# Block 1 of a retention kernel computed as one chunk of 128 tokens, with the order of all steps written anew

## The chip, the cores and the metric

The kernel runs on one core of a Trainium2 chip. The metric is the device time of one execution in microseconds; lower is better. Three runs of the kernel before gave 430.15, 433.15 and 433.55 us, median 433.15. The profile is of one further execution, which took 432.04 us, with a span of 430.3 us from the program's first instruction to its last.

## The reference

Two stages follow each other. The first is a decayed linear attention (retention) over 4 batches, 8 heads, 768 tokens and 64 channels per head, written in the reference with blocks of 64 tokens:

```python
for b in range(nb):                          # nb = 12 blocks of 64
    intra = einsum('bhic,bhjc->bhij', qb, kb) * Dmask        # lam^(i-j) for i >= j
    intra = einsum('bhij,bhjd->bhid', intra, vb)
    inter = einsum('bhid,bhde->bhie', qb * lam_pow, kv_state)  # lam^(i+1)
    out[:, :, sl] = intra + inter
    kb_dec = kb * lam ** (block - 1 - pos)
    kv_state = lam ** block * kv_state + einsum('bhsd,bhse->bhde', kb_dec, vb)
```

The second mixes each token with the one before it (`xk = mu_k * x + (1 - mu_k) * x_prev`, the same for `xr`), and computes `sigmoid(xr @ w_r) * (relu(xk @ w_k)^2 @ w_v)` with a model width of 512 and a hidden width of 1024. The weights come in 64-bit floats, and all results are in 32-bit floats. The block length of the first stage is free: any chunk length gives the same values if the decay tables fit it.

## The kernel before

The 768 tokens go through in NT = 6 blocks of 128, the 8 heads in HP = 4 head pairs. One letter stands for each kind of step, then the block and the head pair or column group; a long string, `ORDER` (lines 483 to 508), lists all steps, and line 459 runs them in this order. Every engine keeps its own instructions in the order in which they are issued (`InOrder`, line 22), so the string sets the order on all five engines and on the load queue, which SyncE (SP) issues. Each engine works in order; a step waits for the data and the buffers that it needs.

Steps of the first stage, per block n and head pair hp:

- `L` (`load_hp`, line 93) and `N` (`load_qv`, line 100) load into one of two input tiles, `IN[hp % 2]`, which head pairs 0 and 2, and 1 and 3, share in turn. Columns 0 to 3 of a tile hold queries, values, keys by column and keys by row. In block 0 one transfer of 1 MB brings all four. In later blocks one of 512 KB brings the keys (`kk`) and two of 256 KB bring queries and values (`qv`); `M` (`clear`, line 108) sets to zero the halves of the tile that must be empty.
- `A` (`scores`, line 249): products of keys and queries into the `sc` tiles in PSUM. `a` (`decay`): VectorE multiplies them by the decay table `Dt` into the tile `mv`.
- `q` (`decay_queries`, line 288): VectorE scales the queries by the table `LP` into other rows of `mv`, in four instructions of 64x256. `k` (`decay_keys`): ScalarE scales the keys in place.
- `U` (`sums`): products of keys and values into `u`. `u` (`even_state`) and `w` (`odd_state`): the state `ST[hp]` is multiplied by a power of the decay and `u` is added; before each, ScalarE copies the state into the empty half of the value columns (`to_values`, line 319; four copies of 64x256 per pair and block).
- `B` (`values`, line 339): values times `mv` into `xp`, from which ScalarE and VectorE make the mixed inputs (`E`, `e`, `F`, `f`).

Block 0 treats its 128 tokens as one chunk: `scores` makes 8 products of 64 rows and 128 columns, `values` 8 products with a stationary tile of 128 rows by 64 columns and 128 moving columns; there is no state yet. Blocks 1 to 5 work in two halves of 64 tokens. The trick there is that the state is laid next to the values of the half, and the scaled queries next to the scores, so that one product of 128 rows gives intra and inter together: 8 products for `scores`, 16 of 64 moving columns for `values`, 8 for `sums`.

Steps of the second stage: `R` and `Q` (the sigmoid branch, two batches each), `s` (sigmoid), `K` (hidden products for one of 8 column groups), `h` and `p` (square and split), `V` (output products, two halves for each batch), `o` (output). Weights are loaded (`S`) as 64-bit numbers and turned to 32 bits on ScalarE, GpSimd and VectorE (`c`, `C`); for blocks 1 to 5 they are split in a high and a low part (`D`, and `x`, `y` for inputs), and each product is made of three quick passes. In block 0 the `R`, `Q` and `K` steps use one slow 32-bit product. `T0`, `T1` and `T2` (`powers`, line 155) make the tables `Dt` and `LP` by products, and `Z` steps (`keep_busy`, line 175) are filler products on zeros.

On TensorE a profile row counts two records for one 32-bit product.

Of the kernel before, what the change touches and what calls it, by code (L numbers as in the profile page):

```python
# [7 lines left out]
F32 = mybir.dt.float32  # L8
# [7 lines left out]
HP = H // 2  # L16
# [17 lines left out]
def tile_retention_moe(  # L34
    ctx: ExitStack,
    tc: tile.TileContext,
    qvk0: bass.AP,
# [50 lines left out]
    LP = const.tile([128, H, 64], F32, name="LP")  # L88
    LC = tiny.tile([128, HP], F32, name="LC")
# [3 lines left out]
    def load_hp(n, hp):  # L93
        t = IN[hp % 2]
        if n == 0:
            sync.dma_start(t[:, 0:4].rearrange("p c o -> p (c o)"), qvk0[hp])
            return
        sync.dma_start(t[:, 2:4].rearrange("p c o -> p (c o)"), kk[n - 1, hp])

    def load_qv(n, hp):  # L100
        t = IN[hp % 2]
        for i in range(2):
            rows, cols = slice(i * 64, i * 64 + 64), slice(i * 4, i * 4 + 2)
            sync.dma_start(t[rows, cols].rearrange("p c o -> p (c o)"), qv[n - 1, hp, rows])
# [3 lines left out]
    def clear(n, hp):  # L108
        t = IN[hp % 2]
        gpsimd.memset(t[64:128, 0 if n == 1 and hp < 2 else 1:2], 0.0)  # L110
        gpsimd.memset(t[0:64, 4 if n == 1 and hp < 2 else 5:6], 0.0)
# [6 lines left out]
    smalls = tiny.tile([128, 7 + H + 2 * HP], F32, name="smalls")  # L118
    sync.dma_start(smalls, small)
    rows = [work.tile([128, w], F32, tag="rt", name="rows", bufs=4) for w in (328, 200)]  # L120
    eye = rows[0][:, 200:328]
    sync.dma_start(rows[0], hot)
    lcol, ecol, lrow, erow, prow = (smalls[:, a:b] for a, b in ((0, 1), (1, 5), (5, 13), (13, 14), (14, 15)))
    mus = smalls[:, 7 + H:].rearrange("p (w c) -> p w c", w=2)
# [7 lines left out]
    lone = work.tile([128, 640], F32, tag="kf", name="lone")  # L132
    gpsimd.memset(lone[:, 512:640], 1.0)
# [13 lines left out]
    rows = rows[1]  # L147
    vector.tensor_scalar(omu, mus, -1.0, 1.0, op0=ALU.mult, op1=ALU.add)
# [6 lines left out]
    def powers(step):  # L155
        i = int(step[1])
        if i == 2:
            by_head = lone[:, 0:512].rearrange("p (h i) -> p h i", h=H)
            vector.tensor_tensor(by_head, rows[:, 72:136].rearrange("p (o i) -> p o i", o=1).broadcast_to([128, H, 64]),
                                 eye[:, 15::16].rearrange("p (h o) -> p h o", o=1).broadcast_to([128, H, 64]), op=ALU.mult)  # L160
            tensor.matmul(tables[2], lone[:, 512:640], lone[:, 0:512], start=True, stop=True)
            scalar.copy(LP.rearrange("p h i -> p (h i)"), tables[2])
            for ab in range(2):
                half = slice(ab * 64, ab * 64 + 64)
                gpsimd.tensor_copy(LC[half], LP[half, :, 63].rearrange("p (h a) -> p a h", a=2)[:, ab])
            return
# [82 lines left out]
    def scores(n, hp):  # L249
        q = Q[hp % 2]  # L250
        if n == 0:
# [19 lines left out]
    def decay(n, hp):  # L271
        sc, mv = scs.pop((n, hp)), mv_of(n, hp)
        if n == 0:
# [14 lines left out]
    def decay_queries(n, hp):  # L288
        q, mv = Q[hp % 2], mv_of(n, hp)
        for eo in range(2):  # L290
            dr = slice(64, 128) if eo == 0 else slice(0, 64)
            for ab in range(2):
                rows = slice(ab * 64, ab * 64 + 64)
                lp = LP[rows, 2 * hp + ab:2 * hp + ab + 1, :].broadcast_to([64, B, 64])
                vector.tensor_tensor(mv[dr, eo, :, ab, :], q[rows, ab, :, eo, :], lp, op=ALU.mult)

    def decay_keys(n, hp):
        kn = KN[hp % 2]
        for ab in range(2):
            h = 2 * hp + ab  # L300
            scalar.activation(kn[:, :, ab, :], kn[:, :, ab, :], AF.Copy, scale=(PW if n == 0 else KD)[:, h:h + 1])

    def sums(n, hp):
        kn, vs = KN[hp % 2], VS[hp % 2]
        us[n, hp] = u = ps_1.tile([128, B, 2, 64], F32, tag="u", name="u")
        for b in range(B):
            for ab in range(2):
                if n == 0:
# [14 lines left out]

    def even_state(n, hp):
        u, state = us[n, hp][:, :, 0, :], ST[hp]
        if n == 0:
            scalar.copy(state, u)
            return
        to_values(n, hp, 0, state)
        vector.scalar_tensor_tensor(state, state, LC[:, hp:hp + 1], u, op0=ALU.mult, op1=ALU.add)  # L330
        to_values(n, hp, 1, state)

    def odd_state(n, hp):
        vector.scalar_tensor_tensor(ST[hp], ST[hp], LC[:, hp:hp + 1], us.pop((n, hp))[:, :, 1, :],
                                    op0=ALU.mult, op1=ALU.add)

    def values(n, hp):
# [4 lines left out]
        for eo in range(1 if n == 0 else 2):  # L342
            for b in range(B):
                for ab in range(2):
                    rows = slice(ab * 64, ab * 64 + 64)
                    if n == 0:
                        tensor.matmul(xp[rows, b].rearrange("p e i -> p (e i)"), vs[:, 0, b, ab, :], mv[:, ab, b, :], start=True, stop=True)
# [136 lines left out]
Sr0 cr0 Cr0 Z10 T0 L00 Sr1 Z1 A00 k00 U00 a00 Z2 B00 cr1 L01 u00 Cr1 Sr2 k01 A01 a01 E00 U01 cr2 L02 u01 e00 T1 B01  # L484
Sr3 E01 L03 T2 F00 k02 Cr2 A02 f00 R00 e01 cr3 a02 U02 B02 M10 k03 u02 F01 f01 A03 Cr3 U03 Sk0 e02 R01 E02 a03 ck0 N10
L10 L11 Q00 f02 F02 R02 u03 Sk1 k10 q10 B03 N11 M11 Ck0 U10 E03 A10 Sk2 F03 Q01 R03 Q02 L12 e03 f03 ck1 u10 a10 B10
Sk3 N12 w10 Sv0 Sv1 M12 k11 U11 A11 s00 Ck1 Q03 s01 q11 E10 e10 ck2 k12 f10 u11 s02 K00 h00 a11 F10 A12 B11 M13 w11
L13 E11 Ck2 e11 a12 ck3 U12 K01 u12 f11 N13 K02 k13 s03 F11 Ck3 K03 w12 x10 cv0 A13 q12 B12 h01 h02 p00 h03 E12 N20
Sv2 Cv0 cv1 a13 L20 Dv0 U13 K04 u13 K05 Cv1 q13 K06 h04 p01 Dv1 K07 Sv3 M20 cv2 w13 A20 k20 U20 V00 h05 y10 L21 Cv2
k21 F12 e12 f12 V02 B13 h06 cv3 Dv2 M21 u20 Cv3 p02 N21 w20 h07 Dv3 p03 y11 x11 Dr0 V04 V06 q20 Dr1 U21 A21 V01 E13  # L490
V03 e13 V05 V07 o00 o01 a20 F13 f13 Dk0 B20 o02 o03 L22 y13 x12 R10 Q10 R11 Q11 R12 Q12 N22 u21 a21 x13 y12 Dk1 R13
Q13 L23 s10 q22 K10 s11 M22 E20 q21 K11 e20 s12 s13 w21 f20 F20 k22 U22 h10 A22 x20 Dk2 B21 K12 M23 a22 Dk3 K13 K14
h11 e21 N23 E21 F21 K15 h12 K16 p10 f21 h13 k23 u22 w22 B22 h14 U23 x21 A23 K17 p11 h15 E22 F22 u23 w23 V10 h16 y20
# [68 lines left out]
```

## Time and profile before

| | |
|---|---|
| runs, median (lowest to highest) | 433.15 us (430.15 to 433.55) |
| profiled execution | 432.04 us, span 430.3 us |
| granted TensorE clock, mean | 1.0 of full speed |
| TensorE matmul busy (records) | 419.5 us, 98% of the span (2935) |
| VectorE | 264.0 us, 61% |
| ScalarE | 204.9 us, 48% |
| GpSimd | 71.0 us, 16% |
| read from memory, written | 35.83 MB, 6.29 MB |

A profile row of a timeline gives the start in us from the span's beginning, the length in us, the engine, the line (all rows say L30, a helper), the operation, the tile written and those read, then for products the stationary tile's rows*columns, the output's partitions x columns, the count of records, and in brackets the idle time before it with what ended it. PE is TensorE's matmul, DVE VectorE, ACT ScalarE, POOL GpSimd, SPq SyncE's load queue. A grouped row gives after the bar the busy us in all, the mean ns of one, and the engine's idle time before such rows. A row of a window gives the stretch, its length, and busy us with the number of instructions for TensorE matmul, its weight loads, VectorE, ScalarE and GpSimd, then clock, share and GB/s of the transfers. Of matmuls the end is modelled, so the distance from one group's start to the next group's start is what it cost.

### The profile page before, as it was taken

How to read it: one execution, taken by the hardware profiler on the slowest of the kernel's cores; microseconds unless marked ns; L12 is line 12 of the kernel's file. 1: busy time of each engine (PE TensorE's matmuls, PEld its weight loads, DVE VectorE, ACT ScalarE, POOL GpSimd, SP SyncE). 2: the span in 40 equal slices, each digit the busy share in tenths (PEclk: the TensorE clock that was granted, in tenths of full speed). 3: DMA queues.
4: the chain of work that ended last, by engine and by line, in shares of the span. 5: the costliest groups of instructions: out<-in, count | busy, mean ns of one | idle time of the engine just before them, and what ended most of it. 6: DMA issues, size and time to landing. Idle time of an engine off the chain costs nothing.

```text
span 430.3 us, 7314 instructions
## 1 busy us (share of the span) xinstructions
PE 419.5 (98%) x2935; PEld 328.9 (76%) x2935; DVE 264.0 (61%) x402; ACT 204.9 (48%) x357; POOL 71.0 (16%) x142
## 2 busy tenths in 40 slices
PE   7998899999999999999999999999999999999996
PEld 4665545668888888888888888888878888888885
DVE  5886999979867674746667646555437561414411
ACT  3645686586677643344644434454244460224300
POOL 4366554331102011110020200000000000000000
PEclk9999999999999999999999999999999999999999
DMA  7889918131403213515004523004520001100001
GB/s 295 304 308 330 300 48 277 66 97 50 146 3 99 87 46 107 153 58 140 0 2 131 187 78 99 0 0 123 161 62 0 2 1 50 50 2 0 0 30 69
DMA packets 12306, 42.60 MB, mean 99 GB/s; under 512 B 1776, under 2 KB 2160, under 8 KB 10736
## 3 DMA queue, kind: packets, MB, share of 16 engines
q1 hardware_dynamic: 8672, 35.84, 26.5%
q10 hardware_dynamic: 3600, 6.29, 4.0%
q8 instruction: 23, 0.38, 0.4%
q14 instruction: 11, 0.09, 0.1%
HBM read 35.83 MB, written 6.29 MB: 98 GB/s over the span
## 4 chain that ended last, share of the span: by engine, by line
PE 81%; DVE 7%; DMA 6%; ACT 2%; POOL 1%; issue 1%; SPq 0%; DVEq 0%; ACTq 0%
PE vp L30 29%; PE kp L30 26%; PE rp L30 13%; PE xp L30 5%; PE sc L30 4%; DMA wst<-w_k 4%; PE u L30 3%; DMA in<-qv 2%; DVE wst L30 2%; DVE mv L30 1%; DVE lov L30 1%; PE table L30 1%; ACT wu L30 1%; DVE wu L30 1%; POOL wu L30 1%
## 5 line engine op out<-in xcount | busy, mean ns | idle before, releaser
L30 PE MATMUL vp<-hiv,k 128*128 128x512 f32 (+1 forms) x400 | 122.8, 384 | 1.0 <-ACT kf L30 1.0
L30 PEld LDWEIGHTS vp<-hiv,k 128*128 128x128 f32 x400 | 74.1, 188 | 16.9 <-ACT kf L30 1.4
L30 PE MATMUL vp<-lov,k 128*128 128x512 f32 (+1 forms) x200 | 76.2, 381 | 0.0
L30 PE MATMUL kp<-xh,hik 128*128 128x512 f32 x160 | 62.9, 393 | 0.0
L30 PE MATMUL kp<-xl,hik 128*128 128x512 f32 x160 | 62.3, 389 | 0.0
L30 PE MATMUL kp<-xh,lok 128*128 128x512 f32 x160 | 62.3, 389 | 0.0
L30 ACT ACTIVATE ts<-xp,omu 128x512 f32<-128x512 f32 x48 | 31.8, 684 | 62.5 <-PE xp L30 44.2
L30 DVE TENSOR_TENSOR kf<-kp,kf 128x512 f32<-128x512 f32 x40 | 27.4, 688 | 37.2 <-ACT kf L30 37.1
L30 ACT ACTIVATE kf<-kp 128x512 f32<-128x512 f32 x48 | 28.4, 594 | 37.6 <-PE kp L30 37.2
L30 ACT COPY in<-st 64x256 f32<-64x256 f32 x80 | 32.3, 404 | 22.1 <-DVE st L30 17.8
L30 PEld LDWEIGHTS vp<-lov,k 128*128 128x128 f32 x200 | 37.6, 188 | 6.9
L30 DVE TENSOR_TENSOR mv<-sc,Dt 64x512 f32<-64x512 f32 (+1 forms) x48 | 32.6, 686 | 12.3 <-PE sc L30 11.9
L30 DVE TENSOR_TENSOR xl<-ts,xh 128x512 fp32r<-128x512 f32 x40 | 27.7, 703 | 19.3 <-ACT xh L30 19.2
L30 DVE SCALAR_TENSOR_TENSOR ts<-xp,smalls,ts 128x512 f32<-128x512 f32 x40 | 29.6, 747 | 15.8 <-ACT ts L30 15.6
L30 DVE TENSOR_TENSOR mv<-in,LP 64x256 f32<-64x256 f32 x80 | 34.5, 431 | 3.2 <-DMA in<-qv 1.6
L30 DVE TENSOR_TENSOR k<-kf,k 128x1024 fp32r<-128x1024 f32 x24 | 29.1, 1223 | 10.7 <-ACT k L30 10.7
L30 DVE TENSOR_TENSOR rt<-vp,rt 128x512 f32<-128x512 f32 (+1 forms) x25 | 16.4, 665 | 31.5 <-PE vp L30 31.2
L30 PEld LDWEIGHTS kp<-xh,hik 128*128 128x128 f32 x160 | 30.0, 188 | 7.0 <-issue 0.9
L30 PEld LDWEIGHTS kp<-xh,lok 128*128 128x128 f32 x160 | 30.0, 188 | 6.3
L30 PEld LDWEIGHTS kp<-xl,hik 128*128 128x128 f32 x160 | 30.0, 188 | 6.0
L30 ACT CAST xh<-ts 128x512 fp32r<-128x512 f32 x40 | 24.1, 616 | 21.7 <-DVE rt L30 18.2
L30 DVE SCALAR_TENSOR_TENSOR st<-st,LC,u 128x256 f32<-128x256 f32 x36 | 17.2, 478 | 24.8 <-ACT in L30 20.0
(70 smaller groups left out, 586.3 us busy)
## 6 DMA issues: line engine op xcount, KB each, us to landing
in<-qv SPq DMA_DIRECT2D x40, 256.0 KB, 4.5
in<-kk SPq DMA_DIRECT2D x20, 512.0 KB, 4.6
out<-rt ACTq DMA_DIRECT2D x23, 256.0 KB, 2.0
in<-qvk SPq DMA_DIRECT2D x4, 1024.0 KB, 6.3
wst<-w_k SPq DMA_DIRECT2D x4, 1024.0 KB, 9.2
wst<-w_v SPq DMA_DIRECT2D x4, 1024.0 KB, 9.7
wst<-w_r SPq DMA_DIRECT2D x4, 512.0 KB, 7.1
out<-rt ACTq DMA_DIRECT2D x2, 128.0 KB, 1.7
```

The source lines that it names most:

```text
L30: return lambda *args, **kw: self.tc.keep_in_program_order(op(*args, **kw))
```

## The change

Block 1 is computed as block 0 is, as one chunk of 128 tokens, and adds what comes from the state by products of its own.

- **Loads.** The array `qvk` holds blocks 0 and 1; `L1x` is one transfer of 1 MB per head pair, and `N1x`, `M1x` are gone. The first clearing of both halves moves to block 2.
- **Scores, sums, decay.** In the forms of block 0. `scores` of block 1 takes two `sc` tiles instead of one.
- **Queries.** One VectorE instruction of 128x512 scales the queries in place, by `LP`, which is now laid out by head pair with 128 powers; `T2` makes it with another stationary tile (`pair`), and one VectorE instruction of 128x1 puts in the last power. Two GpSimd copies that made `LC` are gone; the state update reads its power from `LP`.
- **Values.** For each batch and head: one product as in block 0, then one with the stationary state (64 rows by 64 columns) and the scaled queries, added in PSUM. That is 8 + 8 products of 128 columns per pair.
- **State.** One VectorE instruction in place of two, and the four copies of `to_values` are gone in block 1.
- **Order.** The whole string `ORDER` is another one; two fillers (`Z2`) are gone.

```diff
     def load_hp(n, hp):
         t = IN[hp % 2]
-        if n == 0:
-            sync.dma_start(t[:, 0:4].rearrange("p c o -> p (c o)"), qvk0[hp])
-            return
-        sync.dma_start(t[:, 2:4].rearrange("p c o -> p (c o)"), kk[n - 1, hp])
+        if n < 2:
+            sync.dma_start(t[:, 0:4].rearrange("p c o -> p (c o)"), qvk[n, hp])
+            return
+        sync.dma_start(t[:, 2:4].rearrange("p c o -> p (c o)"), kk[n - 2, hp])
...
-        gpsimd.memset(t[64:128, 0 if n == 1 and hp < 2 else 1:2], 0.0)
+        gpsimd.memset(t[64:128, 0 if n == 2 and hp < 2 else 1:2], 0.0)
...
-    rows = [work.tile([128, w], F32, tag="rt", name="rows", bufs=4) for w in (328, 200)]
+    rows = [work.tile([128, w], F32, tag="rt", name="rows", bufs=4) for w in (456, 200)]
...
     def decay_queries(n, hp):
-        q, mv = Q[hp % 2], mv_of(n, hp)
+        q = Q[hp % 2]
+        if n == 1:
+            q = q[:, 0].rearrange("p b e i -> p b (e i)")
+            vector.tensor_tensor(q, q, LP[:, hp:hp + 1].broadcast_to([128, B, 128]), op=ALU.mult)
+            return
+        mv = mv_of(n, hp)
...
     def even_state(n, hp):
...
+        if n == 1:
+            vector.scalar_tensor_tensor(state, state, LP[:, hp, 127:128], u, op0=ALU.mult, op1=ALU.add)
+            return
...
     def values(n, hp):
...
-                    if n == 0:
-                        tensor.matmul(xp[rows, b].rearrange("p e i -> p (e i)"), vs[:, 0, b, ab, :], mv[:, ab, b, :], start=True, stop=True)
+                    if n < 2:
+                        x = xp[rows, b].rearrange("p e i -> p (e i)")
+                        tensor.matmul(x, vs[:, 0, b, ab, :], mv[:, ab, b, :], start=True, stop=n == 0)
+                        if n == 1:
+                            tensor.matmul(x, ST[hp][rows, b], Q[hp % 2][rows, 0, b].rearrange("p e i -> p (e i)"), start=False, stop=True)
...
 ORDER = """
-Sr0 cr0 Cr0 Z10 T0 L00 Sr1 Z1 A00 k00 U00 a00 Z2 B00 cr1 L01 u00 Cr1 Sr2 k01 A01 a01 E00 U01 cr2 L02 u01 e00 T1 B01
+Sr0 cr0 Z10 T0 L00 Z1 A00 L01 k00 T2 Sr1 U00 a00 B00 Sr2 Cr0 k01 A01 cr1 u00 U01 L02 E00 a01 e00 F00 T1 u01 Sr3 Cr1
```

What the order moves, at three places. First, the values of block 1's first pair on TensorE. Before, `xp` from `mv` and the input tile, between sigmoid products (`rp`) and the next pair's `u` and `sc`:

```order
L30 MATMUL rp<-wr_296,x_6_94 128x512 x2
L30 MATMUL xp<-mv,in_104 64x64 x16
L30 MATMUL u<-in_105 64x128 x8
L30 MATMUL sc<-in_105 64x128 x8
L30 MATMUL rp<-wr_296,x_7_95 128x512 x2
```

In the change, the first five rows of that place (`st_106` is the state of pair 0):

```order
L30 MATMUL rp<-wr_324,x_7_95 128x512 x4
L30 MATMUL sc<-in_105 128x128 x8
L30 MATMUL xp<-mv,in_104 64x128
L30 MATMUL xp<-in_104,st_106 64x128
L30 MATMUL xp<-mv,in_104 64x128
```

The sixteen equal products in a row have become eight of one kind and eight of another, by turns; two key products (`kp`) follow, then the second pair's `u` and its values.

Second, TensorE before the third pair of block 0 (`in_104` for the second time), where the table product of `T2` stood:

```order
 L30 MATMUL xp<-mv,in_105 64x128 x8
-L30 MATMUL table<-lone 128x512
+L30 MATMUL rp<-wr_216,x_4_92 128x512 x2
 L30 MATMUL sc<-in_104 128x128 x8
-L30 MATMUL rp<-wr_156,x_4_92 128x512 x2
 L30 MATMUL u<-in_104 64x64 x8
+L30 MATMUL rp<-wr_216,x_5_93 128x512 x2
 L30 MATMUL xp<-mv,in_104 64x128 x8
 L30 MATMUL sc<-in_105 128x128 x8
```

Two sigmoid products now stand ahead of the scores that need this pair's load; the table product stands between `A00` and `U00`, where the fillers were near.

Third, the load queue from the third key weight on. Before, with the third pair's keys (`kk`) and its queries and values (`qv`) apart:

```order
L30 DMA wst<-w_k 128x2048
L30 DMA in_104<-kk 128x1024
L30 DMA wst<-w_k 128x2048
L30 DMA in_104<-qv 64x1024 x2
L30 DMA wst<-w_v 128x2048 x2
```

In the change:

```order
L30 DMA wst<-w_k 128x2048
L30 DMA wst<-w_v 128x2048
L30 DMA in_104<-qvk 128x2048
L30 DMA wst<-w_v 128x2048 x2
L30 DMA in_105<-qvk 128x2048
```

The third pair has one transfer, behind the last key weight and the first value weight; it needs the whole input tile of the first pair free.

More of the change, by code (lines that the diff above doesn't have):

```diff
@@ L36, in tile_retention_moe @@
     tc: tile.TileContext,
-    qvk0: bass.AP,
+    qvk: bass.AP,
     kk: bass.AP,
@@ L341, in values @@
         xp = pool.tile([128, B, 2, 64], F32, tag=tag, name="xp")
-        for eo in range(1 if n == 0 else 2):
+        for eo in range(1 if n < 2 else 2):
             for b in range(B):
@@ L489 @@
[L489 to L493, printed above, removed]
```

94 lines of the change are left out of this document (48 added, 46 removed).

## The prediction

> **What bounds the kernel now.** I read the page's busy times and slices first.
>
> ```profile
> PE 419.5 (98%) x2935; PEld 328.9 (76%) x2935; DVE 264.0 (61%) x402; ACT 204.9 (48%) x357; POOL 71.0 (16%) x142
> PE   7998899999999999999999999999999999999996
> DVE  5886999979867674746667646555437561414411
> GB/s 295 304 308 330 300 48 277 66 97 50 146 3 99 87 46 107 153 58 140 0 2 131 187 78 99 0 0 123 161 62 0 2 1 50 50 2 0 0 30 69
> ```
>
> TensorE (PE) is busy 98% of the span, from the second slice to the last but one. The loads run at some 300 GB/s through the first five slices, and VectorE (DVE) is at 0.9 in slices four to six only. So I ask stretch by stretch what PE loses.
>
> ```profile
> 40.00:60.00 20.00, 18.37 (x156) 10.90 (x157) 18.91 (x26) 14.54 (x29) 12.11 (x15) 1.00 0.79 249
> 60.00:80.00 20.00, 20.00 (x105) 9.99 (x103) 19.51 (x24) 16.59 (x26) 10.58 (x7) 1.00 0.54 184
> 80.00:100.00 20.00, 19.01 (x155) 15.02 (x154) 16.40 (x20) 12.35 (x19) 6.32 (x7) 1.00 0.20 54
> 200.00:250.00 50.00, 50.00 (x374) 41.56 (x373) 34.67 (x57) 24.89 (x48) 6.66 (x21) 1.00 0.31 96
> ```
>
> DVE is nearly full from 40 to 80 us (18.91 and 19.51 of 20), but PE is busy too (18.37 and 20.00); past 100 us PE has no idle time at all. PE's timeline names each loss before that, in brackets:
>
> ```profile
> 10.90 0.61 PE L30 MATMUL idle<-zeros 128*128 128x512 bf16 x2
> 11.43 1.21 PE L30 MATMUL xp<-mv,in 128*64 128x128 f32 x16
> 18.90 1.16 PE L30 MATMUL sc<-in 64*128 64x128 f32 x16 [0.51 <-DMA in<-qvk]
> ...
> 39.99 1.41 PE L30 MATMUL xp<-mv,in 128*64 128x64 f32 x32 [1.35 <-DVE mv L30]
> 41.40 1.09 PE L30 MATMUL u<-in 128*64 128x128 f32 x16
> 50.30 1.09 PE L30 MATMUL sc<-in 128*64 128x128 f32 x16 [1.59 <-DMA in<-qv]
> 51.20 1.13 PE L30 MATMUL xp<-mv,in 128*64 128x64 f32 x32
> 52.13 1.07 PE L30 MATMUL u<-in 128*64 128x128 f32 x16
> 53.13 10.57 PE L30 MATMUL kp<-x,wk 128*128 128x512 f32 x24
> ...
> 93.04 0.50 PE L30 MATMUL vp<-hiv,k 128*128 128x512 f32 x1 [0.99 <-ACT kf L30]
> ```
>
> Four waits: 0.51 us for a pair's load at 18.9, 1.35 us for VectorE at 40.0, 1.59 us for a load at 50.3, 0.99 us for ScalarE at 93.0. The products after the second trickle in (41.40 - 39.99 = 1.41 us, where the next pair takes 52.13 - 51.20 = 0.93), which is 0.48 more. The two filler products at 10.9 take 11.43 - 10.90 = 0.53 us, from start to the next group's start, as all prices below are taken. Together 0.51 + 1.35 + 0.48 + 1.59 + 0.99 + 0.53 = 5.45 us. **That is the whole prize**: VectorE and ScalarE instructions that go are worth nothing beyond it, and every nanosecond of PE work added from 50 us on is paid in full.
>
> **The change on VectorE, ScalarE and GpSimd.** Its removals, per head pair of block 1:
>
> ```profile
> L30 DVE TENSOR_TENSOR mv<-in,LP 64x256 f32<-64x256 f32 x80 | 34.5, 431 | 3.2 <-DMA in<-qv 1.6
> L30 ACT COPY in<-st 64x256 f32<-64x256 f32 x80 | 32.3, 404 | 22.1 <-DVE st L30 17.8
> L30 DVE SCALAR_TENSOR_TENSOR st<-st,LC,u 128x256 f32<-128x256 f32 x36 | 17.2, 478 | 24.8 <-ACT in L30 20.0
> L30 DVE TENSOR_TENSOR xl<-ts,xh 128x512 fp32r<-128x512 f32 x40 | 27.7, 703 | 19.3 <-ACT xh L30 19.2
> ```
>
> Four scalings of 431 ns become one of 128x512 (nearest row 703 ns): 1.0 us. One state update goes (0.48) and four copies of 404 ns (1.6 us of ScalarE). That is 6 us of VectorE over four pairs, and block 1's clearings move to block 2. All of it lies beside PE work, so I book it only as what lets the waits go. The new scaling in place must wait until the scores have read the queries, and on VectorE the next weight conversion queues behind it; between a pair's scores and its values stand, in the new order, 10 us of sigmoid-branch products for pair 0 and six key products for pair 2, so PE waits for neither.
>
> **The waits.** The 0.51 us: sigmoid products, 1.8 us, now stand ahead of the third pair's scores, as the order shows. The 1.35 + 0.48 us had this chain:
>
> ```profile
> 36.73 1.15 ACT L30 ACTIVATE wu<-wst 128x1024 f32<-128x1024 f32 x1 [1.44 <-DMA wst<-w_k]
> 37.91 0.83 ACT L30 COPY in<-st 64x256 f32<-64x256 f32 x2
> ...
> 90.61 0.82 ACT L30 COPY in<-st 64x256 f32<-64x256 f32 x2 [0.88 <-DVE st L30]
> ```
>
> ```profile
> 38.77 0.48 DVE L30 SCALAR_TENSOR_TENSOR st<-st,LC,u 128x256 f32<-128x256 f32 x1 [2.63 <-ACT in L30]
> ```
>
> Block 1's decay stood behind the state, that behind two copies, these behind a weight's exponent whose load was late. The copies no longer exist, so this goes. The 1.59 us: the third pair's queries were issued at 40.7 and were needed by PE at 48.7, with two weight transfers beside them:
>
> ```profile
> 40.70 1.20 SPq L30 DMA_DIRECT2D in<-qv  x2
> 41.95 1.05 SPq L30 DMA_DIRECT2D wst<-w_v  x2
> ```
>
> ```profile
> in<-qvk SPq DMA_DIRECT2D x4, 1024.0 KB, 6.3
> ```
>
> Now one 1 MB transfer, 6.3 us by its row, waits for the whole of pair 0's values, but its scores stand behind two key products and pair 1's values, over 10 us later: hidden. The 0.99 us came from a ScalarE queue that held copies of block 2's state (at 90.61, waiting for VectorE) ahead of the square; the square now stands ahead, and VectorE has less: it goes. The table of constants grows by 128 columns, 64 KB, at 295 GB/s: +0.2.
>
> **PE's work in block 1.** The shapes of block 0, which block 1 takes over, have their prices in the trace:
>
> ```profile
> 16.24 1.09 PE L30 MATMUL xp<-mv,in 128*64 128x128 f32 x16
> 17.26 1.13 PE L30 MATMUL table<-lone 128*128 128x512 f32 x2
> 21.90 0.69 PE L30 MATMUL u<-in 128*64 128x64 f32 x16
> 22.42 1.04 PE L30 MATMUL xp<-mv,in 128*64 128x128 f32 x16
> 23.39 1.16 PE L30 MATMUL sc<-in 64*128 64x128 f32 x16
> 24.48 0.69 PE L30 MATMUL u<-in 128*64 128x64 f32 x16
> 25.10 5.42 PE L30 MATMUL rp<-wr,x 128*128 128x512 f32 x12
> 30.45 1.09 PE L30 MATMUL xp<-mv,in 128*64 128x128 f32 x16
> ```
>
> Sums of keys and values: before, 53.13 - 52.13 = 1.00; in block 0's form 25.10 - 24.48 = 0.62: -0.38 x 4 = -1.5. Scores: before, 51.20 - 50.30 = 0.90; now 24.48 - 23.39 = 1.09: +0.19 x 4 = +0.8. Values: before 0.93 x 4 = 3.7. New: eight products of 128 rows by 64 columns cost 23.39 - 22.42 = 0.97, and eight of 64 rows by 64 columns from the state alternate with them one by one. No row of before has that. What it has are changes of shape between groups:
>
> ```profile
> 304.11 1.09 PE L30 MATMUL sc<-in 128*64 128x128 f32 x16
> 305.13 0.68 PE L30 MATMUL u<-in 64*64 64x64 f32 x16
> ```
>
> ```profile
> 304.92 0.28 PE L30 MATMUL sc<-in 128*64 128x128 f32 x2
> ```
>
> Scores of 128x64 followed by another 128x64 group take 0.90 (above); followed by a 64x64 group, 305.13 - 304.11 = 1.02. The last two records begin at 304.92 and the next shape at 305.13. **A change costs 0.10 to 0.12 us at its end**, and at its start 0.05: 17.26 - 16.24 = 1.02 behind another shape, 0.97 behind its own. It also forbids two products at a time, which the 64-column groups live on: 12 records of 512 columns, six products, take 30.45 - 25.10 = 5.35, so 0.22 per 128 columns, while the group of eight takes (0.97 - 0.10) / 8 = 0.11 each. A lone product between two changes is therefore 0.22 + 0.10 + 0.05 = 0.37; without the start, 0.32. Sixteen per pair: 5.1 to 5.9 us. The floor, if nothing drains and neighbours overlap, is 16 x 0.11 + 0.2 = 2.0; alone but undrained, 16 x 0.22 = 3.5. I take 5.5, between the two upper prices, as the change's rows are nearest: they show the very pair of shapes, 128x64 and 64x64, and only the length of the run differs.
>
> Block 1's first load is tight. It is issued when block 0's third values are done: 17.26 + two sigmoid products 1.8 + scores 1.1 + sums 0.6 + two more 1.8 + values 1.0 = 23.6; landing 6.3 later, 29.9. PE comes to its scores after scores 1.1, sigmoid 1.8, sums 0.6 and sigmoid 1.8: 28.9. Between 0 and 1.0, I take 0.5.
>
> [...]
>
> **The sum**, on the profiled execution's 432.04 us (span 430.3, and 1.7 around it; 1.1 under the median 433.15): values +22.0 - 3.7, sums -1.5, scores +0.8, waits and filler -5.45, load of pair 0 +0.5, constants +0.2, and three fewer shape changes in the order after block 1, -0.3. That is +12.55: **444.6 us**. With 5.1 per pair 443, with 5.9 446; with half the waits still there, up to 449. In short, time = 422.6 + 4 x values of a pair.
>
> **Rivals.** (1) *The two products overlap*, because a product on rows 0 to 63 and the next pair's product use different columns. For it: records of equal shape start in couples. Against: the couples stop at each change of shape. At 2.0 us a pair the end is 422.6 + 8.0 = 430.6, not slower; it decides below (433.15 - 422.6) / 4 = 2.6 us a pair. (2) *Half-way*: the products are serial, but PE drains little inside one accumulation, 3.5 us a pair: 436.6, slower by under 1%. (3) *New waits besides*: since a pair's state update waits for its slower values, and VectorE's in-order queue with the value weights' conversion stands behind it, PE would stand before the second halves of block 0's value products. My addition of rows along VectorE's new order ends the last such split only a microsecond before PE asks for it. A slip of one conversion, three instructions of 0.7 to 1.2 us, costs 3 us: 447.6.
>
> **How the numbers follow.** Forecast 0.62, rival 3 0.13, rival 2 0.10, rival 1 0.15. About 1% is what a measurement tells from no change, 428.8 to 437.5 here. Slower: forecast and rival 3, 0.75. Same: rival 2 and two thirds of rival 1, 0.20. Faster: the last third of rival 1, 0.05, where the dearer scores and the tight load (0.8 and 0.5) come to nothing as well and a little more is gained than the waits I count. The range runs from rival 1 to beyond rival 3, 430 to 449; the forecast's own is 442 to 447.
>
> **What would show it.** After: values groups of block 1 of 5 to 6 us each with records that no longer start in couples, none of the four waits, VectorE at 0.8 where it was 0.9, and PE idle under 5 us in all. It is wrong if a values group takes under 3 us, or if PE shows waits of over 1 us between 20 and 100 us.

## The result, and the profile after

The changed kernel took 445.75 us in the median of four runs (445.11 to 449.53), the kernel before, beside it, 431.65 us in the median of four (430.02 to 433.55). The ratio is 1.034 with a 95% interval of 1.026 to 1.042: slower. The profiled execution took 445.15 us with a span of 443.4 us, 13.1 us more than the span before.

From the page of the changed kernel, the busy times, two rows of slices and the chain of work that ended last, by line:

```profile
PE 435.7 (98%) x2933; PEld 335.8 (76%) x2933; DVE 254.8 (57%) x387; ACT 199.5 (45%) x341; POOL 64.3 (15%) x131
PE   7999999999999999999999999999999999999996
DVE  4877548658966677646577571777511673613421
PE kp L30 31%; PE vp L30 30%; PE rp L30 15%; PE xp L30 10%; PE sc L30 5%; PE u L30 4%; DMA in<-qvk 1%; PE table L30 1%; DMA rows<-hot 1%; DVE rows L30 1%; DVEq L569 0%; DVE rt L30 0%; SPq L30 0%; PE idle L30 0%; DVE pows L30 0%
```

VectorE's busy time fell by 9.2 us, ScalarE's by 5.4 and GpSimd's by 6.7 (the prediction had counted 6 us on VectorE and 4 x 1.6 on ScalarE). The slices in which VectorE stood at 0.9 before (the fifth to eighth and the tenth; the prediction's words count them as four to six) are now at 0.4 to 0.8, and one at 0.9 is left, the eleventh. TensorE's busy time rose by 16.2 us. The time followed TensorE. Its `xp` products are now 10% of the chain.

The stretches of 20 us, in the columns span, busy time of PE, PEld, DVE, ACT and POOL, granted clock, DMA share and GB/s:

```profile
40.00:60.00 20.00, 20.00 (x111) 10.27 (x110) 9.80 (x12) 7.05 (x12) 7.76 (x8) 1.00 0.52 211
60.00:80.00 20.00, 20.00 (x78) 9.72 (x77) 17.21 (x20) 15.60 (x23) 6.71 (x6) 1.00 0.35 132
80.00:100.00 20.00, 20.00 (x120) 11.53 (x119) 10.90 (x15) 10.09 (x16) 9.70 (x9) 1.00 0.20 54
```

PE has no idle time in any of them, where before it had lost 1.63 us in the first and 0.99 in the last; VectorE does 9.80 where it did 18.91. The granted clock is full. So nothing waits, and the time is longer all the same: it is work.

PE's timeline shows which. The first two rows are the only waits of over 0.1 us after the fillers of the start; the rest is the values group of pair 0 in block 1 with its neighbours, and the ends of that of pair 1:

```profile
7.04 2.00 PE L30 MATMUL table<-rows 128*128 128x64 f32 x16 [0.61 <-DVE rows L30]
...
30.66 1.16 PE L30 MATMUL sc<-in 64*128 64x128 f32 x16 [1.01 <-DMA in<-qvk]
...
40.31 1.16 PE L30 MATMUL sc<-in 64*128 64x128 f32 x16
41.40 0.43 PE L30 MATMUL xp<-mv,in 128*64 128x128 f32 x2
41.76 0.43 PE L30 MATMUL xp<-in,st 64*64 64x128 f32 x2
42.12 0.43 PE L30 MATMUL xp<-mv,in 128*64 128x128 f32 x2
...
47.17 7.13 PE L30 MATMUL kp<-x,wk 128*128 128x512 f32 x16
...
54.75 0.39 PE L30 MATMUL xp<-mv,in 128*64 128x128 f32 x2
...
60.12 0.43 PE L30 MATMUL xp<-in,st 64*64 64x128 f32 x2
60.48 1.16 PE L30 MATMUL sc<-in 64*128 64x128 f32 x16
```

The sixteen products run from 41.40 to 47.17, 5.77 us, in steps of 0.36; those of pair 1 from 54.75 to 60.48, 5.73; the other two pairs take 5.78 and 5.73. Within a product its two records start 160 ns apart, and from the second of them to the next shape there are 200 ns. In a group of one shape the records of two products start within 7 ns of each other (the two at 304.92 in the prediction), such a couple every 0.11 us, so that eight take 0.97 (the prediction's row of block 0); here no product has a neighbour of its own shape, and its records start alone.

The load that pair 0 of block 1 waits for at 30.66, and the transfer of constants:

```profile
24.19 0.33 SPq L30 DMA_DIRECT2D in<-qvk  x1
```

```profile
rows<-hot SPq DMA_DIRECT2D x1, 228.0 KB, 2.8
```

It was issued at 24.5 and its scores began at 30.66. The table of constants took 2.8 us for 228 KB (before, 2.4 for 164 KB), and the first product that needs it starts at 7.04 instead of 6.71.

**Where the 13.1 us come from.** Adding PE's records from start to start, by kind, up to the first quick sigmoid product (110.07 us before, 123.64 now, 13.57 more):

| | us |
|---|---|
| values of block 1: 23.0 instead of 4.35 (0.48 of it trickling) | +18.65 |
| values of block 0 and of block 2's first pair | -0.1 |
| sums of keys and values | -1.8 |
| scores | +0.6 |
| the four waits, without the trickling, and the fillers | -4.97 |
| wait for the load of pair 0 | +1.01 |
| first table product later | +0.33 |
| rest of the sigmoid, key, value and table products | -0.15 |

From there to the end both kernels do the same work, 320.2 us before and 319.8 now.

### The profile page after: what moved, and what is told of

The parts are those of the page before. It is cut to its first block, busy times and chain, and to the rows that moved or that the text cites. A ratio compares the mean times of both kernels' runs of the same rounds, so it can differ in the third digit from the quotient of the medians.

```text
span 443.4 us, 7236 instructions
## 1 busy us (share of the span) xinstructions
PE 435.7 (98%) x2933; PEld 335.8 (76%) x2933; DVE 254.8 (57%) x387; ACT 199.5 (45%) x341; POOL 64.3 (15%) x131
## 3 DMA queue, kind: packets, MB, share of 16 engines
q1 hardware_dynamic: 8032, 35.90, 24.5%
## 4 chain that ended last, share of the span: by engine, by line
PE 96%; DMA 2%; DVE 1%; DVEq 0%; issue 0%; SPq 0%
PE kp L30 31%; PE vp L30 30%; PE rp L30 15%; PE xp L30 10%; PE sc L30 5%; PE u L30 4%; DMA in<-qvk 1%; PE table L30 1%; DMA rows<-hot 1%; DVE rows L30 1%; DVEq L569 0%; DVE rt L30 0%; SPq L30 0%; PE idle L30 0%; DVE pows L30 0%
## 5 line engine op out<-in xcount | busy, mean ns | idle before, releaser
L30 ACT COPY in<-st 64x256 f32<-64x256 f32 x64 | 25.9, 405 | 49.4 <-DVE st L30 24.7
L30 DVE SCALAR_TENSOR_TENSOR st<-st,LP,u 128x256 f32<-128x256 f32 x32 | 15.3, 478 | 45.2 <-ACT in L30 28.0
L30 PE MATMUL xp<-mv,in 128*64 128x64 f32 (+1 forms) x640 | 35.9, 235 | 0.0
L30 PEld LDWEIGHTS xp<-mv,in 128*64 128x64 f32 x640 | 26.4, 137 | 7.3 <-issue 6.2
```

What stands on the lines that cost most here:

```text
L30: return lambda *args, **kw: self.tc.keep_in_program_order(op(*args, **kw))
```

## Experiments

Theory A: the price is the change of shape between a 128x64 and a 64x64 product, paid at each change, with the loss of the neighbour that could run at the same time. Theory B, its rival for the same 5.77 us: the second product adds to what the first has just written, and each add waits for the one before it. B would hit any order in which the two follow each other, whatever their shapes. Two more rivals stand in the expectations of e1: theory C, that products of 64 rows are slow in themselves, and that the new order of the steps costs the time, and not these products. A third question runs beside them: what the lighter VectorE is worth once the products cost less.

**e1_snake: the same sixteen products, sorted into five groups of one shape.** In every odd batch the state's product starts the sum and the scores' product ends it.

```diff
+        for b, state in [(b, (b + i) % 2 == 1) for b in range(B) for i in range(2)] if n == 1 else []:
+            first = state == (b % 2 == 1)
+            for ab in range(2):
+                rows = slice(ab * 64, ab * 64 + 64)
+                x = xp[rows, b].rearrange("p e i -> p (e i)")
+                if state:
+                    tensor.matmul(x, ST[hp][rows, b], Q[hp % 2][rows, 0, b].rearrange("p e i -> p (e i)"), start=first, stop=not first)
+                else:
+                    tensor.matmul(x, vs[:, 0, b, ab, :], mv[:, ab, b, :], start=first, stop=not first)
```

> The same sixteen products of each pair's values in block 1, in another order: two from the scores, four from the state, four from the scores, four from the state, two from the scores, so five groups of one shape in place of sixteen. Theory A (a change of shape costs 0.15 us and forbids two products at a time): 16 x 0.11 + 5 x 0.15 = 2.5 us per pair where the changed kernel shows 5.8, so 445.8 - 4 x 3.3 = 432.7 us. Theory B (a product that adds to what the one before it has just written waits for it): no two neighbours share an output any more, 16 x 0.11 = 1.8 to 2.0 us per pair, 430.5. Theory C (products with 64 rows are slow in themselves, 0.36 us each): 8 x 0.11 + 8 x 0.36 = 3.8 us, 437.9. If the new order of steps is what costs, and not these products: 445.

Measured: 433.32 us in the median (431.65 to 435.94, 10 runs) beside 431.45 of before (429.95 to 434.94, 25 runs); ratio 1.003 (0.999 to 1.006). The profiled execution took 435.9 us. PE's timeline, with its two waits for loads and then the values of pair 0:

```profile
24.65 1.16 PE L30 MATMUL sc<-in 64*128 64x128 f32 x16 [0.70 <-DMA in<-qvk]
...
32.85 2.08 PE L30 MATMUL sc<-in 64*128 64x128 f32 x16 [2.60 <-DMA in<-qvk]
...
45.05 0.44 PE L30 MATMUL xp<-mv,in 128*64 128x128 f32 x4
45.42 0.65 PE L30 MATMUL xp<-in,st 64*64 64x128 f32 x8
46.00 0.66 PE L30 MATMUL xp<-mv,in 128*64 128x128 f32 x8
46.59 0.65 PE L30 MATMUL xp<-in,st 64*64 64x128 f32 x8
47.17 0.44 PE L30 MATMUL xp<-mv,in 128*64 128x128 f32 x4
47.55 7.13 PE L30 MATMUL kp<-x,wk 128*128 128x512 f32 x16
```

The five groups take 0.37, 0.58, 0.59, 0.58 and 0.38 us, 2.50 in all instead of 5.77. Work and operands are the same and so is the number of adds into each accumulator; only the changes of shape went from sixteen to five. Four pairs give back 13.1 us, and the median fell by 12.4. That is A's number. C's 3.8 us a pair and B's 1.8 to 2.0 do not fit it, and neither does a price of the new order of steps, which is still there. But the wait for pair 0's load is now 2.60 us, and the scores behind it last 2.08 us where they last 1.16 elsewhere. The stretches show why, in the column behind the busy times:

```profile
30.00:32.00 2.00, 0.26 (x1) 0.00 (x0) 0.00 (x0) 0.00 (x0) 1.21 (x2) 1.00 1.01 426
34.00:36.00 2.00, 2.00 (x30) 1.77 (x28) 1.02 (x2) 0.00 (x0) 0.00 (x0) 0.50 0.37 156
```

After the wait (in the first of these stretches PE is busy for 0.26 of 2 us) the granted clock is 0.50. From start to start the scores take 2.01 instead of 1.09 us, the sums 0.91 instead of 0.52 and the values 1.12 instead of 0.98: 1.45 us more. **The wait of 2.60 us and the half clock behind it cost 4.05.**

**e2_couples: eight groups of two.** Per batch the two heads' products, then the two from the state.

```diff
-                        if n == 1:
-                            tensor.matmul(x, ST[hp][rows, b], Q[hp % 2][rows, 0, b].rearrange("p e i -> p (e i)"), start=False, stop=True)
+                        for a in range(2 if n == 1 and ab == 1 else 0):
+                            r = slice(a * 64, a * 64 + 64)
+                            tensor.matmul(xp[r, b].rearrange("p e i -> p (e i)"), ST[hp][r, b],
+                                          Q[hp % 2][r, 0, b].rearrange("p e i -> p (e i)"), start=False, stop=True)
```

> The same sixteen products by couples: two from the scores, two from the state, for each batch; eight groups. A: 8 x (0.22 + 0.15) = 2.95 us per pair, 434.5 us. B: 1.8 to 2.0 us, 430.5, the same as with five groups. C: 3.8 us, 437.9.

Measured: 434.64 and 439.14 us, ratio 1.011 (1.001 to 1.021). PE's timeline of the execution of 439.14 us, the fillers of the start and the first table, two of the eight groups and the next kind:

```profile
1.98 4.45 PE L30 MATMUL idle<-zeros 128*128 128x512 bf16 x10 [1.98 <-DVE zeros L30]
6.98 3.68 PE L30 MATMUL table<-rows 128*128 128x64 f32 x16 [0.56 <-DVE rows L30]
...
46.42 0.44 PE L30 MATMUL xp<-mv,in 128*64 128x128 f32 x4
46.79 0.44 PE L30 MATMUL xp<-in,st 64*64 64x128 f32 x4
...
49.36 7.13 PE L30 MATMUL kp<-x,wk 128*128 128x512 f32 x16
```

A group of two takes 0.37 us, so that **a couple costs what a lone product costs** (0.36), and a pair 2.94 (from 46.42 to the next kind at 49.36). A's term is met, B's and C's are not. This execution lost 3.6 us more at its start, which ran at half pace: 3.47 us for the table instead of 1.83 from start to start, and the filler, the scores and the table product behind it 0.25, 0.92 and 0.83 longer. The ten fillers ahead of the table run at half pace too, 0.43 us each where the two at 10.90 before the change took 0.53 together; so they do in the changed kernel (4.45 us). What differs is how long this lasts: in the changed kernel the table at 7.04 already takes 1.84 us from start to start, here the table product at 13.03 still takes 1.89 instead of 1.05.

**e3_same_shape: two adds, one shape.** The state's product is replaced by the scores' product once more, so every accumulator is still written and then added to at once, but no shape changes.

```diff
-                            tensor.matmul(x, ST[hp][rows, b], Q[hp % 2][rows, 0, b].rearrange("p e i -> p (e i)"), start=False, stop=True)
+                            tensor.matmul(x, vs[:, 0, b, ab, :], mv[:, ab, b, :], start=False, stop=True)
```

> Leaves the state's part out of block 1: in place of each product with the state, the product from the scores before it is issued a second time and added, so sixteen products, still each two in a row onto one output, but all of 128 rows by 64 columns. A: no change of shape inside the group, neighbours on different columns overlap, nine steps of 0.22 = 2.0 us per pair, 430.7 us. B: 5.8 us as in the changed kernel, 445.8. C: 2.0 us.

Measured: 431.63 us in the median (430.83 to 435.38, 8 runs), ratio 1.001 (0.997 to 1.005). PE's timeline at the values of pairs 0 and 1:

```profile
42.79 2.02 PE L30 MATMUL xp<-mv,in 128*64 128x128 f32 x32
44.74 7.13 PE L30 MATMUL kp<-x,wk 128*128 128x512 f32 x16
...
53.58 1.99 PE L30 MATMUL xp<-mv,in 128*64 128x128 f32 x32 [1.09 <-DVE ts L30]
```

Sixteen products in 1.95 us (42.79 to 44.74), 0.12 each where the eight of block 0, which add nothing, take 0.12 too (0.97). Adding to a fresh accumulator costs nothing here, and B falls. This kernel leaves out the state and so has other operands; e1, with the operands of the changed kernel, says the same. The price is that of the shapes. With it gone, PE asks for pair 1's accumulator 1.09 us before VectorE has read the old one.

**e4_no_state: what the change would be worth with values at no price.** The state's products are left out.

```diff
-                        tensor.matmul(x, vs[:, 0, b, ab, :], mv[:, ab, b, :], start=True, stop=n == 0)
-                        if n == 1:
-                            tensor.matmul(x, ST[hp][rows, b], Q[hp % 2][rows, 0, b].rearrange("p e i -> p (e i)"), start=False, stop=True)
+                        tensor.matmul(x, vs[:, 0, b, ab, :], mv[:, ab, b, :], start=True, stop=True)
```

> Leaves out the eight products with the state of each pair in block 1 and nothing else. All theories about these products: 1.0 us per pair, 445.8 - 4 x 4.8 = 426.6 us if TensorE is all that counts. If the new order of loads and conversions sets a floor of its own, the time stays above 430 and TensorE shows waits where it had none.

Measured: 431.16 us in the median (428.10 to 433.14, 8 runs), ratio 0.998 (0.994 to 1.003); the profiled execution took 430.31. The median misses the expectation by 4.6 us. PE's timeline of that execution:

```profile
7.63 2.00 PE L30 MATMUL table<-rows 128*128 128x64 f32 x16 [1.20 <-DVE rows L30]
...
32.66 1.16 PE L30 MATMUL sc<-in 64*128 64x128 f32 x16 [0.85 <-DMA in<-qvk]
...
43.39 1.09 PE L30 MATMUL xp<-mv,in 128*64 128x128 f32 x16
44.42 7.25 PE L30 MATMUL kp<-x,wk 128*128 128x512 f32 x16
...
54.14 1.09 PE L30 MATMUL xp<-mv,in 128*64 128x128 f32 x16 [1.85 <-DVE ts L30]
```

The values take 1.03 us (43.39 to 44.42), as expected, 4.7 us per pair less than in the changed kernel. But PE now waits 1.85 us for VectorE's mixing at pair 1's accumulator. In the changed kernel PE gets there 13.35 us after it begins pair 0's values (41.40 to 54.75); here it would after 8.90, and has to stand until 10.75. The slow products had covered that wait. Of the 3.7 us by which this execution exceeds the expectation it is half. The rest is at the start, by this execution's own rows: the first table 0.6 us later (1.20 of waiting instead of 0.61), and behind it a stretch of half clock:

```profile
8.00:10.00 2.00, 2.00 (x18) 1.74 (x19) 0.78 (x2) 0.34 (x1) 0.00 (x0) 0.93 1.00 420
10.00:12.00 2.00, 2.00 (x17) 1.78 (x18) 0.05 (x1) 1.05 (x3) 0.00 (x0) 0.50 0.99 408
```

The scores and the table product in it take 0.92 and 0.66 us longer, though PE is busy throughout. With the 1.85 this comes to 4.0 us, a little more than the 3.7.

**e5_before_moved: the waits without the change.** The kernel before, with one step moved ahead of three of its four waits, to give PE work there: `R00` ahead of block 0's third scores (0.51 us), `Q03` ahead of block 1's first values (1.35), `K01` ahead of its third scores (1.59). The fourth, 0.99 us for ScalarE, was left.

```diff
-Sr3 E01 L03 T2 F00 k02 Cr2 A02 f00 R00 e01 cr3 a02 U02 B02 M10 k03 u02 F01 f01 A03 Cr3 U03 Sk0 e02 R01 E02 a03 ck0 N10
+Sr3 E01 L03 T2 F00 k02 Cr2 R00 A02 f00 e01 cr3 a02 U02 B02 M10 k03 u02 F01 f01 A03 Cr3 U03 Sk0 e02 R01 E02 a03 ck0 N10
...
-L10 L11 Q00 f02 F02 R02 u03 Sk1 k10 q10 B03 N11 M11 Ck0 U10 E03 A10 Sk2 F03 Q01 R03 Q02 L12 e03 f03 ck1 u10 a10 B10
-Sk3 N12 w10 Sv0 Sv1 M12 k11 U11 A11 s00 Ck1 Q03 s01 q11 E10 e10 ck2 k12 f10 u11 s02 K00 h00 a11 F10 A12 B11 M13 w11
-L13 E11 Ck2 e11 a12 ck3 U12 K01 u12 f11 N13 K02 k13 s03 F11 Ck3 K03 w12 x10 cv0 A13 q12 B12 h01 h02 p00 h03 E12 N20
+L10 L11 Q00 f02 F02 R02 u03 Sk1 k10 q10 B03 N11 M11 Ck0 U10 E03 A10 Sk2 F03 Q01 R03 Q02 L12 e03 f03 ck1 u10 a10 Q03 B10 Sk3 N12 w10 Sv0 Sv1 M12 k11 U11 A11 s00 Ck1 s01 q11 E10 e10 ck2 k12 f10 u11 s02 K00 h00 K01 a11 F10 A12 B11 M13 w11
+L13 E11 Ck2 e11 a12 ck3 U12 u12 f11 N13 K02 k13 s03 F11 Ck3 K03 w12 x10 cv0 A13 q12 B12 h01 h02 p00 h03 E12 N20
```

> The kernel before, block 1 in halves, with three steps moved in the order: the first sigmoid products ahead of the third pair's scores of block 0, the last sigmoid products ahead of block 1's first values, the second hidden products ahead of block 1's third scores. TensorE's waits at 18.9, 40.0 and 50.3 us (0.5, 1.8 and 1.6 us) then have work ahead of them. If these waits could be had without the change: 431.5 - 3.9 = 427.6 us. If VectorE, 0.95 busy from 40 to 80 us, sets the pace there, the same time is lost again later, at the output products near 92 us, where it waited 1.0 us: 429.5 to 431 us, with a wait of 2 to 5 us there.

Measured: 432.62 us in the median (432.25 to 435.62, 12 runs) beside 430.81 (430.12 to 433.77, 17 runs); ratio 1.004 (1.001 to 1.006). PE's timeline at its two waits of over 1 us, the stretch of the first, and VectorE ahead of it:

```profile
63.49 0.30 PE L30 MATMUL xp<-mv,in 128*64 128x64 f32 x2 [1.75 <-DVE mv L30]
93.53 0.50 PE L30 MATMUL vp<-hiv,k 128*128 128x512 f32 x1 [1.58 <-ACT kf L30]
```

```profile
60.00:80.00 20.00, 17.94 (x98) 8.99 (x96) 19.48 (x25) 16.53 (x25) 9.44 (x7) 1.00 0.50 184
```

```profile
61.58 1.31 DVE L30 TENSOR_TENSOR xl<-ts,xh 128x512 fp32r<-128x512 f32 x1
62.92 1.77 DVE L30 TENSOR_TENSOR mv<-in,LP 64x256 f32<-64x256 f32 x4
```

The three waits are gone, and others stand in their place: 1.75 us for the scaled queries, whose four instructions VectorE starts at 62.92 behind a weight conversion and a split, and the one for ScalarE has grown to 1.58. VectorE is at 19.48 of 20 us in that stretch. With VectorE this full, more PE work ahead of one wait only brought PE sooner to the next. This speaks for a worth of the lighter VectorE, though not more than the waits; one new order does not show that no other would do without it.

**e6_loads: e1 with pair 0's load earlier in the queue.** Ahead of a weight's transfer, the first key weight's conversion later.

```diff
-B01 f00 L03 R00 E01 cr2 F01 k02 A02 U02 u02 e01 a02 Cr2 cr3 R01 B02 A03 Sk0 L10 Sk1 f01 Q00 Cr3 e02 k03 E02 a03 ck0
-Sk2 U03 u03 Q01 F02 k10 f02 A10 q10 Ck0 U10 B03 E03 F03 R02 e03 Q02 R03 a10 L11 ck1 Q03 s00 s01 f03 A11 Sk3 B10 Ck1
+B01 f00 L03 R00 E01 cr2 F01 k02 A02 U02 u02 e01 a02 Cr2 cr3 R01 B02 A03 L10 Sk0 Sk1 f01 Q00 Cr3 e02 k03 E02 a03 Sk2 U03 u03 Q01 F02 k10 f02 A10 ck0 q10 U10 B03 E03 F03 Ck0 R02 e03 Q02 R03 a10 L11 ck1 Q03 s00 s01 f03 A11 Sk3 B10 Ck1
```

> The five-group kernel with block 1's first load ahead of the first key weight in the load queue, and that weight's conversion placed later on ScalarE, GpSimd and VectorE. The wait of 1.0 to 2.6 us for this load should fall to 0.3 or less: 433.3 - 1.3 = 432.0 us, still no better than before (431.5). If the wait does not come from the transfer ahead but from the moment at which the input tile comes free, it stays and the time with it.

Measured: 437.22 us in the median (435.43 to 439.82, 6 runs); ratio 1.014 (1.009 to 1.018). A miss. The load's issue, PE's waits and VectorE's gap in the profiled execution of 439.4 us:

```profile
28.02 0.33 SPq L30 DMA_DIRECT2D in<-qvk  x1
```

```profile
34.48 1.16 PE L30 MATMUL sc<-in 64*128 64x128 f32 x16 [1.00 <-DMA in<-qvk]
41.71 3.70 PE L30 MATMUL rp<-wr,x 128*128 128x512 f32 x8 [0.95 <-DVE x L30]
58.77 0.44 PE L30 MATMUL xp<-mv,in 128*64 128x128 f32 x4 [1.35 <-DVE ts L30]
```

```profile
40.90 0.75 DVE L30 SCALAR_TENSOR_TENSOR x<-xp,smalls,ts 128x512 f32<-128x512 f32 x1 [4.53 <-POOL ts L30]
```

With no weight's transfer directly ahead of it the load still needs 6.1 us, from the end of its issue at 28.35 to the scores at 34.48. The queue was not its trouble: it is issued 0.15 us after the values that read its tile give way to the next group (27.87 and 28.02 here, 24.04 and 24.19 in the changed kernel), and then takes its time. The weight steps moved behind it cost two new waits for VectorE, 0.95 and 1.35 us: in VectorE's gap of 4.53 us it waits for GpSimd's `ts`, which stands behind the moved conversion in the order (such a conversion takes GpSimd 2.85 us in the mean). This execution also waited 0.91 us for the very first load, and the granted clock was 0.50 from about 9.5 to 16.3 us (0.88 in the mean from 8 to 10 us, 0.50 from 10 to 16, and the values at 15.04 still take 1.61 us instead of 0.98), which cost 2.9 us.

**e7_scores_later: e1 with the scores of block 1 behind more work.** The fourth pair's values and the mixing go first, and two more batches of sigmoid products.

```diff
-Sk2 U03 u03 Q01 F02 k10 f02 A10 q10 Ck0 U10 B03 E03 F03 R02 e03 Q02 R03 a10 L11 ck1 Q03 s00 s01 f03 A11 Sk3 B10 Ck1
+Sk2 U03 u03 Q01 F02 f02 B03 E03 k10 Ck0 F03 R02 A10 q10 U10 e03 Q02 R03 a10 L11 ck1 Q03 s00 s01 f03 A11 Sk3 B10 Ck1
```

> The five-group kernel with block 0's last values and two sigmoid products placed ahead of block 1's first scores on TensorE, and the key scaling of that pair behind the mixing on ScalarE. The load of this pair takes 5 to 6 us from the moment the tile is free, whatever stands ahead of it; with 2.9 us more of products ahead, TensorE's wait of 1.0 to 2.6 us is gone: 433.3 - 1.5 = 431.8 us, about what the kernel before takes. If the wait only moves on (to the conversions behind the scaled queries), 433.

Measured: 433.57 us in the median (431.46 to 436.03, 11 runs) beside 430.62 (429.66 to 434.79, 22 runs); ratio 1.006 (1.003 to 1.009). The profiled one took 431.59 us. Its first table, the only row of PE behind the fillers with a wait in brackets, the scores of block 1's first pair, and one stretch:

```profile
6.85 2.19 PE L30 MATMUL table<-rows 128*128 128x64 f32 x16 [0.41 <-DVE rows L30]
...
32.78 1.16 PE L30 MATMUL sc<-in 64*128 64x128 f32 x16
```

```profile
40.00:60.00 20.00, 20.00 (x156) 11.24 (x157) 15.09 (x19) 12.79 (x20) 12.04 (x10) 1.00 0.73 296
```

The load is hidden: it is issued at 24.18, and PE comes to it 8.6 us later, at 32.78, without a wait. PE waits for nothing from the first table on. This is the change with all that it could win: its span, 429.8 us, is 0.5 under that of before. The values cost 2.5 instead of 0.97 per pair (before's 4.35 without the trickling, by four), +6 us, and this takes the waits' 5.45 us back. In the median it does not beat the kernel before: it is 0.6% above it. Its runs spread over 4.6 us. Half pace, as in e2 (3.6 us) and in the next kernel (2.8), would give such a spread. The run of 436.03 us had a mean granted clock of 0.990, and 1% of its 434 us is up to 4.3 of the 4.4 us by which it exceeds the profiled one; the others have no profile that would tell, so this is argued and not shown.

**e8_pair_later: e7 with the added constants in a transfer of their own,** behind the first pair's load.

```diff
+            if (n, hp) == (0, 0):
+                sync.dma_start(pair, hot[:, 328:456])
...
-    rows = [work.tile([128, w], F32, tag="rt", name="rows", bufs=4) for w in (456, 200)]
-    eye, pair = rows[0][:, 200:328], rows[0][:, 328:456]
-    sync.dma_start(rows[0], hot)
+    rows = [work.tile([128, w], F32, tag="rt", name="rows", bufs=4) for w in (328, 200)]
+    eye, pair = rows[0][:, 200:328], work.tile([128, 128], F32, tag="rt", name="pair", bufs=4)
+    sync.dma_start(rows[0], hot[:, 0:328])
```

> The same, and the 128 columns of constants that the change added are loaded by a transfer of their own behind the first pair's load. The first table product should start 0.2 to 0.3 us earlier, near 6.7 us, if the size of the constants delayed it: 0.2 to 0.3 us off the time, 431.5; at the edge of what five rounds tell. If the first pair's load sets the pace, nothing changes.

Measured: 432.24 us in the median (431.34 to 438.38, 12 runs); ratio 1.004 (1.001 to 1.006). The profiled execution took 435.47 us; its first table and its two transfers of constants:

```profile
8.13 3.68 PE L30 MATMUL table<-rows 128*128 128x64 f32 x16 [1.70 <-DVE rows L30]
```

```profile
rows<-hot SPq DMA_DIRECT2D x1, 164.0 KB, 3.8
pair<-hot SPq DMA_DIRECT2D x1, 64.0 KB, 6.4
```

The table, the filler and the scores behind it run at half pace (1.64, 0.25 and 0.92 us longer, 2.8 in all); as in e2, the pace of the first fillers (4.45 us for ten) lasts on, and the table product at 14.17 is the first group at the full one (1.06 us). The smaller transfer took 3.8 us in this execution, longer than the larger one in the changed kernel, so the profile says nothing on the 0.33 us, and the intervals of e7 and e8 overlap. Over all traces the first table starts at 6.71 and 6.84 us with the smaller constants alone (before and e5), at 6.79 to 7.63 with the larger (the changed kernel, e1 to e4, e6 and e7). The 0.33 of one pair of profiles lies within this spread, so the constants' price is not shown.

## Why the prediction was right, step by step

The forecast was its first case, lone products between two changes of shape, with 444.6 us; the profiled execution took 445.15 and the median is 445.75.

- **Values of block 1**, the large term: 23.0 us against 22.0, 5.77 a pair where 5.5 was taken between 5.1 and 5.9. The step from groups to lone products held: a lone one costs 0.36, near the upper price of 0.37. Choosing a value between the two prices was the error; the price with the change paid at both ends came nearest. In the changed kernel 128x64 and 64x64 products start 0.36 us apart, one by one, where in e2 two of one shape take 0.37 together, and sixteen runs of one shape in place of five are worth 3.27 us per pair (5.77 against e1's 2.50). By an estimate from e1, e2 and e3, about half of this, 11 x 0.15, is the changes themselves, the rest the lost neighbours. The prediction's word for the price is that PE drains; the runs show the price, and none shows what happens in it.
- **The waits**: the four are gone, as each was argued, and nothing took their place but the load. Here the slow values helped. e3 and e4, in which they are quick, wait 1.09 and 1.85 us for VectorE at pair 1's accumulator; at e7's 2.5 us there is no such wait.
- **Load of pair 0**: 1.01 us, the upper bound of 0 to 1.0, where 0.5 was taken. Both ends of the estimate came later by the same 0.75: PE was ready at 29.65 instead of 28.9, the data there at 30.66 instead of 29.9. In e1, e2, e3 and e4 the same wait was 2.60, 1.08, 1.33 and 0.85 us. A bound from one median of four transfers was too narrow for it.
- **Small terms**: the sums gave 1.8 instead of 1.5 us, scores cost 0.6 instead of 0.8, the table came 0.33 later instead of 0.2, the part behind block 1's order gave 0.4 instead of 0.3. Values of before cost 3.87 without trickling, not 3.7, since the fourth group stands between groups of another shape and takes 1.08. The misses partly cancel, so that the total lies nearer (445.15 against 444.6) than its largest term (23.0 against 22.0).
- **VectorE and ScalarE at no price**: right. 9.2 and 5.4 us less work, and no part of it in the time beyond the waits.
- **Rivals**: overlap (2.0 us a pair) is what e3 shows for products of one shape, 1.95; so the rival failed on the shape and not on the adding. The half-way case, 3.5 a pair, is refuted by the 5.77. The slip of a conversion did not occur.

The formula of the prediction, 422.6 plus the values of four pairs, can be held against the other kernels. It gives 445.6 for the changed one (profiled 445.15), 434.4 for e2 (434.64, and 439.14 in the execution that had 3.6 us of half pace and 1.66 more of waits for loads, 1.08 twice in place of 0.5), 432.6 for e1 (median 433.32, profiled 435.9) and for e7 (median 433.57, profiled 431.59), and 430.4 for e3 (median 431.63, profiled 432.53). For e4 it gives 426.7 (median 431.16, profiled 430.31), and there it fails, by the 1.85 us of waiting that the values had covered and by the slow start: a wait that goes is worth its length only as long as no other stands close behind it.

## What to carry to other kernels

Count the changes of shape on TensorE as well as the products: where short products of two shapes alternate, sort them into runs, which an accumulator allows by starting the sum with either, as in e1 (2.50 us a pair instead of 5.77). Where TensorE is busy 98% of the time, a change that relieves another engine can win no more than TensorE's waits, here 5.45 us; add up that prize first, and then look for what it costs TensorE. Before a slow step is made quick, ask what waits it covers (1.85 us in e4).

## What was not expected

- **A lone 32-bit product with 128 moving columns costs as much as two of one shape**: 0.36 against 0.37 us. Four take 0.58, and sixteen without a change 1.95. In runs a product costs about 0.11 and each change about 0.15, worked out from e1, e2 and e3 (16 x 0.11 + 5 x 0.15 = 2.5; 16 x 0.11 + 8 x 0.15 = 2.96). What the change consists of is open: in the changed kernel the weight load of the next shape starts together with its product (41.76), in block 0's group of one shape some 0.1 us ahead of it (22.53 and 22.64), and no run shows whether this late load is what is paid for.
- **A short wait can be followed by half pace for microseconds.** In e1 the granted clock was 0.50 from about 32.7 us, just before a wait of 2.60 ended, to 36.1 (0.67 in the mean from 32 to 34 us, 0.50 from 34 to 36, 0.98 from 36 to 38), which cost 1.45 us. In e4 it was 0.50 from about 9.7 to 13.1 (0.93 in the mean from 8 to 10 us, 0.50 from 10 to 12, 0.86 from 12 to 16), 2.1 us after a wait of 1.20 had ended, and in e6 from about 9.5 to 16.3, behind 0.67 and in the midst of 0.91. That these waits caused it is argued from the order of events alone. In the kernel before, 1.59 us at 50.30 had no such effect, nor had 1.75 us at 63.49 in e5 (granted clock 1.00 in both stretches), so what decides is not the length of the wait alone. The half pace lasted some 3.4 us in e1 and in e4 and twice that in e6; what starts it and what sets its length, no run shows.
- **The start runs at half pace, and its length varies.** The first fillers start 0.43 us apart in the kernel before, the two at 10.90 only 0.23, and the first ten take 3.90 to 4.45 us in all traces. The first table takes 1.83 to 2.02 us from start to start in eight traces, but 3.47 in e2 and e8; the half pace lasts there through the table product at 13.03 (1.89 us instead of 1.05) and the scores at 12.16 (2.01 instead of 1.09), and they lost 3.6 and 2.8 us by it. The column of the granted clock reads 1.00 there all the same (8 to 12 us in both); the pace is then to be read from the rows (3.68 us for 2.00). Why these two stayed slow for so long is open. The losses at half pace, 1.45 to 3.6 us in these executions, are a good part of the prize of this change.
- **The 1 MB load of block 1's first pair took 6.2 to 8.7 us from issue to landing**: 6.3 us in the changed kernel, where the scores that wait for it start 0.14 us after it has landed, and by the same 0.14, 8.7 in e1, 7.6 in e2, 7.7 in e3 and 6.2 in e4, with a weight's transfer directly ahead of it, 6.3 in e6 without. The 5 to 6 us of e7's expectation lie nearer to the pages' medians of all eight such loads, 5.2 to 6.8 us in these kernels. What makes it long is open; the weights' transfers issued behind it keep the DMA engines busy as well (share 1.01 from 30 to 32 us in e1). It can be hidden by needing it later, as in e7, where e1's 8.7 us would have ended at 32.9, just when the scores ask for it (32.78).
